# Attention, gated feed-forward and their product on one core: gate rows in free places, output weights split at the end, shared sums, and a doubled load of x

## The chip, the cores and the metric

The kernel runs on one core of a Trainium2 chip. Five engines work beside each other, each through its own queue of instructions in order: TensorE (PE, with weight loads shown apart as PEld), VectorE (DVE), ScalarE (ACT), GpSimd (POOL) and SyncE (SP), which here issues all DMA transfers. The metric is the device time of one execution in microseconds (us). Before the change it is 2596.14 us, the median of three runs (2592.55 to 2599.0).

## The reference

For x of 2048 tokens with D = 576 values, in float32:

```python
xn = _layernorm(x, axis=-1)
# attention, 32 heads of 18 values: wqkv is (576, 1728), wo is (576, 576)
q, k, v = ...(xn @ wqkv)
p = _softmax(einsum("bhqd,bhkd->bhqk", q, k) * 18 ** -0.5)
s = einsum("bhqk,bhkd->bhqd", p, v).reshape(B, S, D) @ wo
# feed-forward: w_gate and w_up are (576, 4608), w_down is (4608, 576)
y = (_gelu(xn @ w_gate) * (xn @ w_up)) @ w_down
return x + s * _silu(y)
```

## The kernel before

**Precision.** Operands of the matmuls have the type float32r; each is split into a high part and a low part (`split`, `split_ap`, `split_av`, `cut`: a copy gives the high part, a subtraction the low one), and a product is three matmuls: high by high, high by low, low by high.

**Stages.** A prologue normalizes x, transposes it, and projects queries, keys and values, four blocks of 512 tokens (`b`); it writes qk, vs and the transposed x (`xhs`, both parts) to DRAM. In its last block it also splits `wo` and stores the parts in DRAM as `wos` (`split_wo`, `store_wo`, L313 to L323). Then attention and feed-forward run interleaved. The feed-forward is cut into sections: one section is one slice of 128 of the 4608 inner columns for one block of 512 tokens, 27 pairs of matmuls (`gate_up`, L427; a pair is `pg` on partitions 0 to 63 and `pu` on 64 to 127). Two sections make a group `r` (`G` = 2, `NR` = 18 groups per block); after each group follows the down projection `py` (L538, 42 matmuls by a scheme with seven products), which DVE adds to `M` (L545). An attention section carries 8 slots beside the pairs: in each, a score product `pe` (L831) whose exponential ACT takes (L832), and for a later head group a product `pm` (L779) whose maximum DVE takes (L781). `pe`, `pm`, `py` and others share a ring of three PSUM buffers. After the section come 32 matmuls `acc` (L848) with the values.

**A change of block.** The pairs read the transposed x in three thirds of 192 rows, `xd[k]`, each as a high and a low tile, and need it on partitions 0 to 63 and again on 64 to 127. In the last section of a block `load_xd` (L144) loads the lower halves for the next block, and `copy_xd` copies them to the upper halves: ACT the high tiles (L151; the second and third thirds in three pieces each, between the exponentials of the next section), POOL the low tiles (L153). In the same place POOL forms sums of h and splits them (L465 to L467, L455, L456), which the down projection reads, and four pieces of T (the prepared down weights, `t_piece`, L483) are loaded.

**Scaling.** The attention's outputs lie unnormalized in DRAM (`oT`) with reciprocals `rT`. In free places of the attention, for one head group each time, `load_scale`, `scale` and `store_scale` load, multiply on POOL (L705) and store them as `on`. Two of the 32 are left to the end.

**The end.** After the attention five sections and three down projections remain. Among them stand 16 steps, one per 128 rows of the output: `project` (L991, 28 matmuls of the outputs with the parts of `wo`, result `po`), on DVE `multiply` (L1000, the gate row by po; L1005, plus x), then the store; then for a later row `split_o` (ACT `oh` L972, DVE `ol` L973 and L974) and `gate` (ACT tanh L982, DVE L983: y * (tanh(y/4) + 1), of which the product with 0.25 makes a gate, y being held doubled). Gate rows y of the first three blocks come from DRAM (`ys`), those of the last from `M`. `load_o` brings the normalized outputs of a block into KA.

**Order.** PE's instructions stand in the order of the code throughout; SP's from the attention on; ACT's, DVE's and POOL's in the end alone. Elsewhere a scheduler orders them when the program is built, except where `keep_in_program_order` holds one. `spread` places the slots and the `hooks` (work issued at a given pair) among a section's pairs.

Of the kernel before, what the change touches and what calls it, by code (L numbers as in the profile page):

```python
# [17 lines left out]
P = 128  # L18
# [3 lines left out]
KT = 4  # L22
# [30 lines left out]
PRODUCTS = ((2, (0, 6)), (5, (1, 3)), (3, (2, 5)), (6, (3, 4)), (0, (4, 2)), (4, (5, 1)), (1, (6, 0)))  # L53
QUARTERS = ((0, 0, 6), (0, 1, 4), (1, 0, 1), (1, 1, 5))
# [27 lines left out]
def kernel(ctx: ExitStack, tc: tile.TileContext, x, wqkv, wo, w_gate, w_up, w_down, out):  # L82
# [12 lines left out]
    wos = dram.tile([2, D, D], F32, name="wos")  # L95
# [70 lines left out]
    with tc.tile_pool(name="pro", bufs=1) as pro, tc.tile_pool(name="pps", bufs=1, space=PSUM) as pps:  # L166
# [102 lines left out]
        parts = []  # L269
# [42 lines left out]

        def split_wo(k):  # L313
            n = min(P, D - k * P)
            raw = raw_tile([P, D])
            tc.keep_in_program_order(nc.sync.dma_start(raw[0:n], wo[k * P:k * P + n, :]))
            hi, lo = (pro.tile([P, D], F32R, name=f"wo{i}", tag="rawp", bufs=5) for i in range(2))
            split(hi[0:n], lo[0:n], raw[0:n])
            return k, n, hi, lo

        def store_wo(k, n, hi, lo):
            for i, t in enumerate((hi, lo)):
                tc.keep_in_program_order(nc.sync.dma_start(wos[i, k * P:k * P + n, :], f(t)[0:n]))  # L323
# [33 lines left out]
        for b in range(NB):  # L357
            for n, t in enumerate(ORDER):
# [16 lines left out]
                if b == NB - 1 and 2 <= n < NK + 2:  # L375
                    store_wo(*parts.pop(0))
                if b == NB - 1 and n < NK:
                    parts.append(split_wo(n))
# [22 lines left out]
    FF = {"w": ahead, "xd": XD, "down": [], "gates": [], "n": 0, "hooks": {}, "next": {}, "raw": {},  # L401
# [169 lines left out]
    def section(specials=(), tag="f", slots=False, tail=0):  # L571
# [7 lines left out]
        hooks, FF["hooks"], FF["next"] = FF["hooks"], FF["next"], {}  # L579
# [48 lines left out]
    def finish():  # L628
# [8 lines left out]
        def hook(i, what, ahead="hooks"):  # L637
            FF[ahead].setdefault(i, []).append(what)

        def behind(what):  # L640
            if (n + 1) % (NR * G) == 0:
                hook(9, lambda: what(keep))
            else:
                what(lambda i: i)
# [23 lines left out]
        else:  # L668
            if g == 0:
                late = (n + 2) % (NR * G) == 0 and n + 2 < NF  # L670
                for k, i in enumerate((1, 6, 11, 16) if late else (None, 5, 13, 21)):
                    if i is None:
                        t_piece(r, k)
                    else:
                        hook(i, lambda k=k: t_piece(r, k), ("hooks", "next")[late])
# [17 lines left out]
    def load_scale(u):  # L693
# [3 lines left out]
        if not SC:  # L697
            SC.extend(ffn.tile([P, 2, TB], F32, name=m, tag=t) for m, t in (("on", "rawd"), ("od", "tsum")))
        nc.sync.dma_start(SC[0][:, u % 2], oT[g, :, cols])
        nc.sync.dma_start(SC[1][:, u % 2], rT[QD * g:QD * g + QD, cols].rearrange("h (o s) -> h o s", o=1).to_broadcast([QD, 32, TB]))  # L700

    def scale(u):

        o, d = (t[:, u % 2] for t in SC)
        nc.gpsimd.tensor_tensor(o, o, d, op=ALU.mult)  # L705

    def store_scale(u):

        j, g = divmod(u, NQ)
        for a in range(QD):  # L710
            row = (QD * g + a) * DH
            nc.sync.dma_start(on[j][row:row + DH, :], SC[0][32 * a + 1:32 * a + 1 + DH, u % 2])
# [9 lines left out]
    with tc.tile_pool(name="att", bufs=1, reuse_waits="tile") as att:  # L722
# [185 lines left out]
        scaled = 0  # L908
# [248 lines left out]
```

## Time and profile before

| | us |
|---|---|
| median of three runs | 2596.14 |
| profiled execution | 2595.73 |
| its span | 2593.9 |
| PE busy | 2554.1 (98%) |
| DVE busy | 2111.7 (81%) |
| POOL busy | 1599.7 (62%) |
| ACT busy | 1468.6 (57%) |

The span goes from the first to the last instruction; the profiled execution took 1.83 us more. Times of the trace count from the span's start. A row of the timeline is: start, duration, engine, line, operation, output and inputs, and in brackets how long the engine had been idle and what released it. Of the 2593.9 us the prologue and the first sections take about 340, the interleaved attention goes to about 2456, and the end takes the rest.

### The profile page before, as it was taken

Reading aid. Unit: us, or ns where it says so; the run is one execution under the profiler, and the core shown is the slowest. Engines: PE = TensorE matmul, PEld = TensorE weight load, DVE = VectorE, ACT = ScalarE, POOL = GpSimd, SP = SyncE. Lnnn points to the kernel's source line nnn. Section 1 sums busy time; section 2 is a strip of 40 time slices with the busy share of each in tenths; the row PEclk is TensorE's granted clock in tenths of the full one; section 3 lists DMA queues with packets and bytes.
Section 4 is the critical chain, followed back from the end, with each engine's and each line's share of the span. In section 5 each row is a group of like instructions: output and inputs, shape, how many; then the busy total and the mean of one; then the engine's idle time right before and its main releaser. Section 6 shows DMA issues by size and latency. Waiting matters only on the chain.

```text
span 2593.9 us, 52857 instructions
## 1 busy us (share of the span) xinstructions
PE 2554.1 (98%) x20548; PEld 1847.5 (71%) x20548; DVE 2111.7 (81%) x2399; ACT 1468.6 (57%) x1769; POOL 1599.7 (62%) x1679
## 2 busy tenths in 40 slices
PE   9999999999999999999999999999999999999988
PEld 8887766666666777666666676666666666676778
DVE  5325888888888888888878988888887888887377
ACT  3224366666666666555566655555566555556521
POOL 2115588888888855666667665555557655556641
PEclk9999999999999999999999999999999999999998
DMA  8865455555565566666666666666557665554683
GB/s 264 266 237 147 109 166 152 167 164 161 167 188 164 165 170 165 159 165 166 167 174 172 168 167 162 161 160 157 155 151 213 163 156 150 153 155 134 187 255 126
DMA packets 407880, 442.87 MB, mean 171 GB/s; under 512 B 106700, under 2 KB 286412, under 8 KB 407632
## 3 DMA queue, kind: packets, MB, share of 16 engines
q1 hardware_dynamic: 407632, 439.50, 61.6%
q8 instruction: 163, 2.67, 0.4%
q14 instruction: 85, 0.70, 0.1%
HBM read 344.12 MB, written 95.26 MB: 169 GB/s over the span
## 4 chain that ended last, share of the span: by engine, by line
PE 92%; DVE 2%; DMA 2%; POOL 1%; ACT 1%; issue 1%; SPq 1%; POOLq 0%; DVEq 0%; ACTq 0%
PE pg L427 27%; PE acc L848 17%; PE py L538 14%; PE pe L831 9%; PE pm L779 9%; PE po L187 7%; PE pu L427 7%; PE py L525 1%; PE po L991 1%; DMA raw<-in_B_w_up_dram 0%; DMA wol<-wos 0%; DVE mx L781 0%; DMA KA<-on 0%; PE pt L248 0%; DMA yy<-ys 0%
## 5 line engine op out<-in xcount | busy, mean ns | idle before, releaser
L832 ACT ACTIVATE pT<-pe 128x1024 f32<-128x1024 f32 x1024 | 1049.0, 1027 | 586.0 <-PE pe L831 551.1
L781 DVE TENSOR_REDUCE mx<-pm 128x2 f32<-128x1024 f32 x1024 | 1220.5, 1224 | 176.6 <-PE pm L779 161.8
L427 PE MATMUL pu<-xd,wh 64*128 64x512 f32 x2538 | 927.5, 397 | 6.5 <-POOL xd L153 4.9
L427 PE MATMUL pg<-xd,wh 64*128 64x512 f32 x2538 | 926.0, 396 | 1.9 <-ACT t L440 1.9
L427 PEld LDWEIGHTS pg<-xd,wh 64*128 64x128 f32 x2538 | 468.6, 185 | 123.7 <-issue 57.0
L427 PE MATMUL pg<-xd,wl 64*128 64x512 f32 x1269 | 496.4, 391 | 1.2 <-POOL wl L117 1.2
L427 PE MATMUL pu<-xd,wl 64*128 64x512 f32 x1269 | 495.9, 391 | 0.0
L427 PEld LDWEIGHTS pu<-xd,wh 64*128 64x128 f32 x2538 | 468.5, 185 | 24.4 <-POOL xd L153 5.7
L110 POOL TENSOR_SCALAR wh<-raw 128x384 fp32r<-128x384 f32 x402 | 215.4, 537 | 437.4 <-PE pu L427 333.4
L848 PE MATMUL acc<-pT,VS 128*32 128x512 f32 x4096 | 466.0, 595 | 0.0
L112 POOL TENSOR_TENSOR wl<-raw,wh 128x384 fp32r<-128x384 f32 x402 | 413.4, 1031 | 28.6
L779 PE MATMUL pm<-KA,QT 64*128 64x512 f32 x2048 | 416.5, 394 | 5.6 <-ACT pT L832 3.6
L831 PE MATMUL pe<-QT,KA 64*128 64x512 f32 x2048 | 412.5, 392 | 2.2 <-DVE mx L781 1.9
L538 PE MATMUL py<-T,ah 128*128 128x288 f32 x1876 | 385.9, 301 | 9.9 <-DVE yy L1000 7.0
L545 DVE TENSOR_TENSOR M<-py,M 128x576 f32<-128x576 f32 x448 | 338.8, 758 | 31.2 <-PE py L538 18.5
L538 PEld LDWEIGHTS py<-T,ah 128*128 128x128 f32 x1876 | 302.0, 190 | 65.9 <-issue 61.5
L456 POOL TENSOR_TENSOR al<-h,ah 128x512 fp32r<-128x512 f32 (+1 forms) x142 | 292.8, 2062 | 52.6 <-ACT ah L453 42.5
L848 PEld LDWEIGHTS acc<-pT,VS 128*32 128x32 f32 x4096 | 120.3, 109 | 276.5 <-issue 229.5
L538 PE MATMUL py<-T,al 128*128 128x288 f32 x938 | 277.8, 296 | 0.0
L831 PEld LDWEIGHTS pe<-QT,KA 64*128 64x128 f32 x2048 | 194.3, 184 | 113.0 <-DVE mx L781 26.2
L427 PEld LDWEIGHTS pg<-xd,wl 64*128 64x128 f32 x1269 | 234.4, 185 | 38.4 <-POOL wl L117 2.0
L427 PEld LDWEIGHTS pu<-xd,wl 64*128 64x128 f32 x1269 | 234.7, 185 | 8.3
(156 smaller groups left out, 2908.4 us busy)
## 6 DMA issues: line engine op xcount, KB each, us to landing
T<-ts SPq DMA_DIRECT2D x98, 576.0 KB
KA<-qk SPq DMA_DIRECT2D x768, 72.0 KB
T<-ts SPq DMA_DIRECT2D x98, 432.0 KB
raw<-in_B_w_gate_dram SPq DMA_DIRECT2D x144, 288.0 KB
raw<-in_B_w_up_dram SPq DMA_DIRECT2D x144, 288.0 KB
ts<-T SPq DMA_DIRECT2D x36, 576.0 KB
VS<-vs SPq DMA_DIRECT2D x128, 152.0 KB
qk<-t SPq DMA_DIRECT2D x72, 256.0 KB
```

Source lines behind the costliest of these rows:

```text
L110: first = nc.gpsimd.tensor_scalar(hi, raw, 1.0, 1.0, op0=ALU.mult, op1=ALU.mult)
L112: keep(nc.gpsimd.tensor_tensor(lo, raw, f(hi), op=ALU.subtract))
L187: nc.tensor.matmul(o, st, m, start=(i == 0), stop=(i == len(terms) - 1))
L427: nc.tensor.matmul(o, w[1 + wp][k][rr, c, :], xd[k][xp][rr, c, :], start=(i == 0), stop=(i == len(terms) - 1))
L456: keep(two.tensor_tensor(lo, raw, f(hi), op=ALU.subtract))
L538: nc.tensor.matmul(py[:, t, 0:DC], h[:, i, tt], T[:, w, k], start=n == 0, stop=n == 2)
L545: nc.vector.tensor_tensor(M[:, m], py[:, :, 0:DC], M[:, m], op=ALU.add)
L779: nc.tensor.matmul(pm[:, a], QS[u, r][rr, t * P:(t + 1) * P], KS[(u * NA + c) % KB][r][rr, :], start=True, stop=True)
L781: return nc.vector.tensor_reduce(MX[u][:, 2 * r:2 * r + 2, t, c], pm, axis=AX.X, op=ALU.max)
L831: nc.tensor.matmul(pe[:, a], KS[(u * NA + c) % KB][r][rr, t * P:(t + 1) * P], QS[u, r][rr, :], start=True, stop=True)
L832: nc.scalar.activation(PT[u, kt][:, 2 * r:2 * r + 2, :], pe, AF.Exp, scale=SCALE)
L848: nc.tensor.matmul(ACC[u][32 * a:32 * a + 32, :], VS[(u * NA + c) % VB][:, v:v + 32], pt[:, a, :], start=first, stop=last, skip_group_chec ...
```

## The change

1. **Output weights.** `wos` goes, with `split_wo` and `store_wo` in the prologue. At the end `load_wo` loads `wo` as it is into tiles that later hold x and gate rows, ACT copies the high parts, POOL subtracts the low ones.
2. **x at a change of block.** The last third is loaded twice, into both halves; its copies on ACT and POOL go. POOL's copies of the second third stand ahead of the sums of h, whose hook goes. Before the second and third change, two pieces of T are loaded ahead of x, two right behind it.
3. **Gate rows in the attention.** Where no scaling is ready, a place takes a gate row: load from `ys`, tanh on ACT, a multiplication and a sum on POOL, store to `ys`. Eleven of the twelve rows of the first three blocks are gated so; `gate` in the end does the twelfth.
4. **The end.** Both left scalings are loaded first and done in one place; x is loaded seven rows ahead; the sum with x goes to POOL in every second step up to the tenth; all pieces of T for the second down projection are loaded ahead of the steps. One projection moves from ahead of the last section to behind it: four, section, three, down, one, section, three, down, instead of four, section, three, down, two, section, two, down.

```diff
-    def load_xd(b, k):
+    def load_xd(b, k, halves=1):
             t = wts.tile([P, XG, TB], F32R, name=f"xd{i}_{k}")
-            nc.sync.dma_start(f(t)[0:HR], xhs[b][i, k * XG * HR:(k + 1) * XG * HR, :].rearrange("(k p) t -> p k t", p=HR))
+            for a in range(halves):
+                nc.sync.dma_start(f(t)[HR * a:HR * a + HR],
+                                  xhs[b][i, k * XG * HR:(k + 1) * XG * HR, :].rearrange("(k p) t -> p k t", p=HR))
...
         if new:
-            xd.append(load_xd(b + 1, NG - 1))
-            for k in range(1, NG):
-                for i in range(XG):
-                    FF["hooks"].setdefault(7 * k + 2 * i - 5, []).append(lambda k=k, i=i: copy_xd(xd[k], 0, keep, i))
-            for k in range(NG):
+            xd.append(load_xd(b + 1, NG - 1, 2))
+            for t in hooks.get(len(pairs), ()):
+                t()
+            for i in range(XG):
+                FF["hooks"].setdefault(2 + 2 * i, []).append(lambda i=i: copy_xd(xd[1], 0, keep, i))
+            for k in range(NG - 1):
                 for i in range(XG):
                     copy_xd(xd[k], 1, keep, i)
...
         def behind(what):
-            if (n + 1) % (NR * G) == 0:
-                hook(9, lambda: what(keep))
-            else:
-                what(lambda i: i)
+            what(keep if (n + 1) % (NR * G) == 0 else lambda i: i)
...
-                for k, i in enumerate((1, 6, 11, 16) if late else (None, 5, 13, 21)):
+                for k, i in enumerate((None, 5, 27, 27) if late else (None, 5, 13, 21)):
...
+    def gate(k, i):
+        y, t = (t[:, i] for t in SC)
+        nc.scalar.activation(t, y, AF.Tanh, scale=0.25)
+        nc.gpsimd.tensor_tensor(t, t, y, op=ALU.mult)
+        nc.gpsimd.tensor_tensor(y, y, t, op=ADD)
...
-            if FF["n"] % G == 1 and (scaled + 1) * NA + 4 < n and SCALED <= n < NU * NA - 2 and 2 < FF["n"] % (NR * G) < NR * G - 2:
-                load_scale(scaled)
-                at(n + 1, 2, scale, scaled)
-                at(n + 2, 0, store_scale, scaled)
-                scaled += 1
+            if FF["n"] % G == 1 and SCALED <= n < NU * NA - 2 and 2 < FF["n"] % (NR * G) < NR * G - 2:
+                done = scaled + gated
+                if (scaled + 1) * NA + 4 < n:
+                    jobs, k = (load_scale, scale, store_scale), scaled
+                    scaled += 1
+                else:
+                    jobs, k = (load_gate, gate, store_gate), gated
+                    gated += 1
+                jobs[0](k, done % 2)
+                at(n + 1, 2, jobs[1], k, done % 2)
+                at(n + 2, 0, jobs[2], k, done % 2)
...
         def load_wo():
-            nc.gpsimd.memset(f(OW[1])[HR:P, KT, :], 0.0)
-            for i, w in enumerate(OW):
-                nc.sync.dma_start(f(w)[:, 0:KT, :], wos[i, 0:R0, :].rearrange("(k p) n -> p k n", p=P))
-                for a in range(2 - i):
-                    nc.sync.dma_start(f(w)[HR * a:HR * a + HR, KT, :], wos[i, R0:D, :])
+            for i, t in enumerate(RAW[:KT]):
+                nc.sync.dma_start(t, wo[i * P:(i + 1) * P, :])
+            for a in range(2):
+                nc.sync.dma_start(RAW[KT][HR * a:HR * a + HR], wo[R0:D, :])
+
+        def split_wo():
+            wh, wl = OW
+            pool.memset(f(wl)[HR:P, KT, :], 0.0)
+            for i, t in enumerate(RAW):
+                act.activation(wh[:, i], t, AF.Copy)
+                rr = slice(0, P if i < KT else HR)
+                pool.tensor_tensor(wl[rr, i], t[rr], f(wh)[rr, i], op=SUB)
...
-            vec.tensor_tensor(xx, xx, t, op=ADD)
+            (pool if k % 2 and k < SHARED else vec).tensor_tensor(xx, xx, t, op=ADD)
```

`RAW` is `XX + YY[2:]`, three tiles for x and two for gate rows; `SHARED` is 11; `SC` holds the two buffers of the scaling, which the gate rows share.

ACT at the third change of block, before and after (`pT` are exponentials, `xd_1` and `xd_2` the second and third thirds of x, the numbers behind them those of the tiles):

```order
L852 ACTIVATE accs<-acc 128x512
L832 ACTIVATE pT<-pe 128x1024
L151 ACTIVATE xd_1_24419<-xd_1_24419 64x512
L832 ACTIVATE pT<-pe 128x1024
L151 ACTIVATE xd_1_24419<-xd_1_24419 64x512 x2
L832 ACTIVATE pT<-pe 128x1024
L151 ACTIVATE xd_2_24475<-xd_2_24475 64x512
L832 ACTIVATE pT<-pe 128x1024
L151 ACTIVATE xd_2_24475<-xd_2_24475 64x512 x2
L832 ACTIVATE pT<-pe 128x1024 x4
```

```order
L853 ACTIVATE accs<-acc 128x512
L833 ACTIVATE pT<-pe 128x1024
L153 ACTIVATE xd_1_24397<-xd_1_24397 64x512
L833 ACTIVATE pT<-pe 128x1024
L153 ACTIVATE xd_1_24397<-xd_1_24397 64x512 x2
L833 ACTIVATE pT<-pe 128x1024 x6
```

Three of six copies between the exponentials are gone; the other three stay where they were.

POOL at the second change of block, before and after (`h` are the activations whose sums and splits `ah`, `al` the down projection reads; `wh` and `wl` the split weights of later sections):

```order
L153 COPY xd_0_16593<-xd_0_16593 64x512 x3
L465 TENSOR_TENSOR h_16682<-h_16436,h_16682 128x512
L466 TENSOR_TENSOR h_16682<-h_16436,h_16682 128x256
L467 TENSOR_TENSOR h_16682<-h_16682 128x256
L455 TENSOR_SCALAR ah<-h_16682 128x1280
L456 TENSOR_TENSOR al<-h_16682,ah 128x1280
L153 COPY xd_1_16636<-xd_1_16636 64x512 x3
L110 TENSOR_SCALAR wh<-raw 128x384
L112 TENSOR_TENSOR wl<-raw,wh 128x384
L153 COPY xd_2_16692<-xd_2_16692 64x512 x3
```

```order
L155 COPY xd_0_16550<-xd_0_16550 64x512 x3
L155 COPY xd_1_16593<-xd_1_16593 64x512 x3
L450 TENSOR_TENSOR h_16639<-h_16391,h_16639 128x512
L451 TENSOR_TENSOR h_16639<-h_16391,h_16639 128x256
L452 TENSOR_TENSOR h_16639<-h_16639 128x256
L110 TENSOR_SCALAR wh<-raw 128x384
L440 TENSOR_SCALAR ah<-h_16639 128x1280
L112 TENSOR_TENSOR wl<-raw,wh 128x384
L441 TENSOR_TENSOR al<-h_16639,ah 128x1280
```

The copies of the second third went ahead of the sums, those of the last third are gone. In the attention, ten of the eleven tanh (`od<-on`) stand behind the fourth or fifth of a section's eight exponentials, one ahead of the first.

DVE in the end, two steps between the second section and the second down projection, before and after (`yy` gate rows, `po` the projection, `xxs` rows of x, `ol` and `oh` parts of a later step's outputs):

```order
L1000 SCALAR_TENSOR_TENSOR yy_31013<-yy_31013,po 128x576
L1005 TENSOR_TENSOR xxs<-xxs,yy_31013 128x576
L973 TENSOR_TENSOR ol<-KA,oh 128x512
L974 TENSOR_TENSOR oh<-KA,oh 64x128
L983 SCALAR_TENSOR_TENSOR yy_31015<-th,yy_31015 128x576
L1000 SCALAR_TENSOR_TENSOR yy_31014<-yy_31014,po 128x576
L1005 TENSOR_TENSOR xxs<-xxs,yy_31014 128x576
L973 TENSOR_TENSOR ol<-KA,oh 128x512
L974 TENSOR_TENSOR oh<-KA,oh 64x128
L983 SCALAR_TENSOR_TENSOR yy_31012<-th,yy_31012 128x576
```

```order
L1015 SCALAR_TENSOR_TENSOR yy_31015<-yy_31015,po 128x576
L990 TENSOR_TENSOR ol<-KA,oh 128x512
L991 TENSOR_TENSOR oh<-KA,oh 64x128
L1015 SCALAR_TENSOR_TENSOR yy_31016<-yy_31016,po 128x576
L1020 TENSOR_TENSOR xxs<-xxs,yy_31016 128x576
L990 TENSOR_TENSOR ol<-KA,oh 128x512
L991 TENSOR_TENSOR oh<-KA,oh 64x128
```

The gate's operation left DVE, and of two sums one.

More of the change, by code (lines that the diff above doesn't have):

```diff
@@ L398 @@
     ps = ctx.enter_context(tc.tile_pool(name="ps", bufs=1, space=PSUM, reuse_waits="tile"))
[L401 removed]
+    FF = {"w": ahead, "xd": XD, "down": [], "gates": [], "n": 0, "hooks": {}, "raw": {},
           "M": ffn.tile([P, 7, 2, DC], F32, name="M"),
@@ L1011, in step @@
             split_o(n + 2)
-            gate(n + 2)
-            load_xy(n + 4)
+            b, j = groups[min(n + 2, len(groups) - 1)]
+            if b < 2 and j == TB // P - 1:
+                load_o(b + 2)
             for t in pieces[:2]:
@@ L1016, in step @@
             del pieces[:2]
+            load_y(n + len(YY))
+            load_x(n + len(XX))
             n += 1
+            if ahead:
+                gate(n + 1)
         def load_raw(n):
@@ L1061 @@
         todo.pop("rec")[0]()
-        split_o(0)
+        for i, u in enumerate(rest):
+            load_scale(u, i)
+        load_wo()
+        for k in range(2):
+            load_y(k)
+        load_raw(first + 3)
         end()
@@ L1091 @@
         cut_a(1, h1, pool, pool)
-        gate(1)
+        load_raw(first + 4)
         for m in ("rawd", "tsum"):
@@ L1095 @@
             XX.extend((t[:, 0], t[:, 1]))
-        load_xy(3)
-        for k in range(2):
-            step()
-        load_raw(first + 4)
-        for k in range(2):
+        for t in pieces:
+            t()
+        del pieces[:]
+        for k in range(3, len(XX)):
+            load_x(k)
+        for k in range(4):
             step()
@@ L1103 @@
         end()
-        for k in range(3):
+        for k in range(2):
             step()
+        step(False)
         last_down(1)
+        gate(n + 1)
         sums_a(0, h, pool)
         cut_a(0, h, pool, pool)
-        for k in range(2):
-            step()
+        step()
         h, end = last_section("f")
```

115 lines of the change are left out of this document (51 added, 64 removed).

## The prediction

> **What bounds the kernel.** First the page's engine table, then the stages of the program with each engine's busy time (columns: stretch, length, busy PE, PEld, DVE, ACT, POOL, granted clock, DMA share, GB/s), then two pieces of the chain that ended last.
>
> ```profile
> PE 2554.1 (98%) x20548; PEld 1847.5 (71%) x20548; DVE 2111.7 (81%) x2399; ACT 1468.6 (57%) x1769; POOL 1599.7 (62%) x1679
> ...
> 150.00:220.00 70.00, 68.85 (x440) 58.63 (x439) 21.66 (x29) 21.37 (x40) 30.49 (x31) 1.00 0.69 219
> ...
> 713.33:751.29 37.96, 34.92 (x279) 23.43 (x279) 29.44 (x30) 27.41 (x33) 30.87 (x34) 1.00 0.78 207
> ...
> 1319.86:1360.41 40.55, 36.85 (x279) 25.96 (x279) 29.19 (x30) 25.38 (x30) 24.37 (x31) 0.92 0.70 179
> ...
> 1925.35:1961.61 36.26, 34.48 (x280) 23.79 (x279) 29.75 (x30) 25.30 (x30) 23.33 (x29) 1.00 0.77 196
> ...
> 2456.37:2594.00 137.63, 118.17 (x845) 108.04 (x844) 101.50 (x135) 29.61 (x44) 41.79 (x38) 0.93 0.63 198
> ```
> ```profile
> 1286.62 5.74 PE py L538 x42
> 1319.86 5.74 PE py L538 x42
> ```
>
> TensorE is the bound: 2554 of 2593.9 us. In the attention the chain returns to the same down projection every 33.24 us, and PE is busy throughout. What is not PE stands in few places: the three changes of token block, called T1, T2 and T3 here, where such a period takes 37.96, 40.55 and 36.26 us, thus 4.7, 7.3 and 3.0 above 33.24; and the last 137.6 us, where PE rests for 19.5 and runs part of the time at a lower granted clock (0.93 on average). So a cost on another engine counts only where PE then waits, and a gain only in those four places.
>
> **Prologue: nothing.** Five splits of the output weights on POOL, ten stores and five loads go. The row 150 to 220 above holds them; PE rests 1.15 us there in all. That is the most to be had; the waits in it stand behind ACT copies whose order does not change, so I take 0 (0 to 1).
>
> **Block changes: 10.6 us.** Two causes stand in the rows: at T2 POOL, at T3 ACT.
>
> ```profile
> 1340.29 1.29 POOL L465 TENSOR_TENSOR h<-h,h 128x512 f32<-128x512 f32 x1 [1.01 <-DVE h L444]
> ...
> 1344.41 2.88 POOL L456 TENSOR_TENSOR al<-h,ah 128x1280 fp32r<-128x1280 f32 x1
> 1347.36 1.73 POOL L153 CAST xd<-xd 64x512 fp32r<-64x512 f32 x3
> ...
> PE pu L427 <- POOL xd L153: 3.6, 1, 3.6
> ```
> ```profile
> 1945.73 1.03 ACT L832 ACTIVATE pT<-pe 128x1024 f32<-128x1024 f32 x1 [0.23 <-PE pe L831]
> 1946.78 0.63 ACT L151 ACTIVATE xd<-xd 64x512 fp32r<-64x512 f32 x1
> ...
> 1956.03 2.14 ACT L832 ACTIVATE pT<-pe 128x1024 f32<-128x1024 f32 x2 [0.48 <-PE pe L831]
> ```
> ```profile
> 1646.42 2.12 ACT L832 ACTIVATE pT<-pe 128x1024 f32<-128x1024 f32 x2 [2.04 <-PE pe L831]
> ...
> 1651.32 2.13 ACT L832 ACTIVATE pT<-pe 128x1024 f32<-128x1024 f32 x2 [0.22 <-PE pe L831]
> 1653.89 2.16 ACT L832 ACTIVATE pT<-pe 128x1024 f32<-128x1024 f32 x2 [0.44 <-PE pe L831]
> ```
>
> At T2 the copies of the second third of x stand on POOL behind the sums and splits of h, 1340.29 to 1347.3, and PE waits 3.6 us for them. In the new order both groups of copies precede the sums. At T3 six copies between the exponentials (3.6 us at 0.6 each) put the seventh exponential 10.30 us behind the first, against 7.47 in an undisturbed section: 2.83 us later, so that ACT hands on all but 0.75 us of what is put between. Three copies remain, 1.8 us, of which I let 1.2 through. So T3 falls from 3.0 to 1.2, T2 from 7.3 to 1.2.
>
> The last third now comes by four transfers in place of two. What that costs the queue:
>
> ```profile
> 1936.00:1947.00 11.00, 11.00 (x97) 6.92 (x95) 8.82 (x10) 9.69 (x12) 6.43 (x11) 1.00 1.02 212
> ...
> xd<-xhs SPq DMA_DIRECT2D x24, 384.0 KB
> ```
>
> Six loads of 384 KB fill the queues for 11 us at 212 GB/s, 1.86 us each. Two more shift the end from about 1947.3 to 1951, with some 2 us to the signal 1953. PE's section there starts at about 1945.0 (the first exponential, 1945.73, needs its first product); two thirds in, with 1.2 us of delay, it asks for the low part at 1953.6 (6.6 us of pairs, two pairs more). So the cover is about 0.6 us at T3, 1 at T2 by the same count, and at T1, where stores of T share the queues, it is gone by 0.8: T1 falls from 4.7 to 2.0. Gain 2.7 + 6.1 + 1.8 = 10.6. Bounds: 12 if the halves load at once, 4 if the last third comes 2 us later still at each change. [...]
>
> Two pieces of T's high part now go ahead of the x loads and two right behind; they had been late at T2 and T3 without a wait of PE, so 0. The sums of h lose a hook and stand behind the copies: at T2 their splits end at 1347.3, one group of copies (1.73) moves ahead of them, and the down that reads them is the one at 1360.41: 0.
>
> **Gating in the attention: a loss of 2.5 us.** Eleven times: one load and one store of 288 KB, a tanh on ACT, two POOL operations. Order: ten tanh stand among the eight exponentials of a section, one ahead of them.
>
> ```profile
> L982 ACT ACTIVATE th<-yy x12: 667/686/692, 2480.9 to 2557.1; 128x576 f32<-128x576 f32 x12
> ...
>   DMA od<-rT: 4.4, 4
> ```
> ```profile
> 747.64 1.43 POOL L490 TENSOR_TENSOR tsum<-rawd 128x576 f32<-128x576 f32 x1
> ...
> 1637.04 1.30 POOL L705 TENSOR_TENSOR on<-on,od 128x512 f32<-128x512 f32 x1
> 1642.20 0.99 POOL L110 TENSOR_SCALAR wh<-raw 128x384 fp32r<-128x384 f32 x2 [3.86 <-PE pu L427]
> ```
>
> A tanh takes 0.69 us. Behind the fourth exponential ACT has 0.22 us free, and 0.44 two later; the fifth ends about 0.5 late. Between nothing (the 0.75 that T3 absorbed) and 0.69 on PE I take 0.25, by the nearest row, the slack at 1651.32: ten times, 2.5 us (0 to 7). POOL: 2.9 us where a multiplication at 1637.04 had 3.86 us free behind it: hidden, and without that cover the next weight splits, not needed for a section, are late. SP's queue: the store waits for POOL half a period after it, nothing is late behind it. In 30 such loads before, POOL waited 4.4 us in all (the row of the tile "on"), so I add no wait for data.
>
> **The end: 14 us.** The stretches of the end, and the chain's price of a projection:
>
> ```profile
> 2456.40:2481.10 24.70, 24.12 (x198) 19.94 (x199) 17.44 (x22) 6.31 (x10) 7.96 (x10) 1.00 1.07 296
> 2481.10:2502.10 21.00, 17.70 (x122) 17.30 (x121) 16.21 (x19) 4.82 (x8) 16.20 (x15) 0.92 0.53 162
> 2502.10:2521.40 19.30, 17.83 (x139) 16.18 (x139) 12.66 (x17) 4.79 (x8) 5.32 (x6) 1.00 1.07 350
> 2521.40:2536.50 15.10, 8.97 (x46) 8.19 (x45) 13.32 (x17) 2.00 (x3) 5.21 (x5) 0.77 0.66 219
> ```
> ```profile
> 2536.49 7.42 PE po L991 x56
> ```
> ```profile
> 2496.84 0.40 PE L991 MATMUL po<-woh,ol 128*128 128x288 f32 x1 [3.30 <-DVE ol L973]
> 2528.28 0.82 PE L538 MATMUL py<-T,ah 128*128 128x288 f32 x2 [4.68 <-DVE yy L1000]
> ```
> ```profile
> 2550.36 0.60 ACT L1040 ACTIVATE h<-pg 128x512 f32<-128x512 f32 x1 [5.10 <-PE pg L427]
> ```
> ```profile
> 2495.04 1.75 DVE L973 TENSOR_TENSOR ol<-KA,oh 128x512 fp32r<-128x512 f32 x1
> ...
> 2556.59 1.49 DVE L456 TENSOR_TENSOR al<-h,ah 128x1280 fp32r<-128x1280 f32 x1 [1.34 <-ACT ah L453]
> 2558.01 0.75 DVE L1000 SCALAR_TENSOR_TENSOR yy<-yy,po 128x576 f32<-128x576 f32 x1
> 2558.79 0.76 DVE L1005 TENSOR_TENSOR xx<-xx,yy 128x576 f32<-128x576 f32 x1
> 2559.46 0.68 DVE L973 TENSOR_TENSOR ol<-KA,oh 128x512 fp32r<-128x512 f32 x1
> 2560.16 0.28 DVE L974 TENSOR_TENSOR oh<-KA,oh 64x128 fp32r<-64x128 f32 x1
> 2560.48 0.76 DVE L983 SCALAR_TENSOR_TENSOR yy<-th,yy 128x576 f32<-128x576 f32 x1
> ```
>
> A projection is 7.42 / 2 = 3.71 us, a down projection 5.74, a section (24.12 - 5.74) / 3 = 6.1. From 2481.1 to 2536.5 PE has seven projections, one section and one down: 26.0 + 6.1 + 5.7 = 37.8 us of work in 55.4, so 17.6 are lost, most of it behind DVE. Per step DVE now does 0.75 + 0.76 + 0.68 + 0.28 + 0.76 = 3.2 us alone and more beside POOL (1.75 for 0.68). The last 0.76 goes for 11 of 12 rows, and every second sum up to the tenth step goes to POOL: 1.7 and 2.5 us per step, below PE's 3.71. What stays: about 2 us where DVE runs beside POOL (first four steps), and 1 in the second down projection, whose first sums wait for a step. So 17.6 falls to about 3.6: 14 us.
>
> The split of the raw weights must fit ahead of the first projection at 2481: 1.44 MB lands, after 1 MB for the scales and the T pieces, at about 2471 at the 296 GB/s of that row or better; ACT 5 x 0.69 from there, POOL 5 x 1.43 beside it, end about 2480. Bounds 0 to 3 us of loss; I take 0, as wol's POOL price is a row, and count 3 in the range. POOL's sums of rows 1 and 3 stand behind its splits of h, near 2496; SP's load of the third block of outputs (KA) waits behind the first of them, until about 2497, and is needed only after three more projections and a section: 0.
>
> From 2536.5 to 2570 the third projection now follows the last section. DVE's chain after that section ends with al 7.7 us behind it (2550.3 to 2558.0); then multiplication, sum and split (0.75 + 0.76 + 0.68) give the fourth projection its operand some 20 us after the down, where PE would be ready at 17.3. T's last pieces come behind the store of the same step, at about 24. Both put the down's start at 24, where it began at 21 but stood half done until 25.6: gain 0 (-3 to +3).
>
> **Rivals.** First, DVE stays the bound of the end: ol and its companion 3.0 us beside POOL in each of seven steps gives 0.75 + 0.38 + 3.0 = 4.1 or, with doubled sums, 4.5 us against 3.71, 5.6 us more, and 2 for late weights: 2582. For it speaks 1.75 against 0.68, against it that POOL is free in half the steps. [...] Second, the last third of x lands late at all three changes: the waits of PE stay by half, gain 4, 2580. Third, slower: tanh waits for its load, and the exponentials queue behind it on ACT, then PE. At 22 us of net gain it takes 3.0 us per gate, ten times, to come out 7.8 us above: 2604. Four waits in 30 loads speak against it. Fourth, both first rivals and full tanh prices together leave less than 7.8 us: 2592.
>
> **Numbers.** 10.6 - 2.5 + 14 = 22 us. The profiled execution took 2595.73 us (span 2593.9 and 1.8 around it), 0.4 below the median of the runs: 2574. Forecast 0.60, first rival 0.16, second 0.10, third 0.06, fourth 0.08. The range goes from full gains (2564) to both rivals (2588). 0.3% is 7.8 us, about what runs of this kernel differ by (2592.6 to 2599.0): faster 0.86, same 0.08, slower 0.06.
>
> **What would show it.** Periods at the changes of about 35.2, 34.4 and 34.4 us; PE waits for POOL's copies gone at T2; sections with a tanh 0.25 longer; the down of 2521 some 14 earlier, with no PE wait above 2 us for yy; the clock at 1.00 there. Wrong if the period in the attention grows by over 0.5 us, or if PE waits for woh or wol.

## The result, and the profile after

The changed kernel takes 2580.95 us, median of four runs (2580.15 to 2582.14), against 2596.7 for the kernel before beside it (2592.55 to 2599.0): a ratio of 0.9941, 95% interval 0.9924 to 0.9959, 15.75 us less. Forecast were 2574 and a range of 2564 to 2588. The profiled execution after took 2580.15 us, with a span of 2578.4, which is 15.5 below the span before.

The span divides best at the down projections, since each period of the attention starts with one. First their starts in the chain of work that ended last, for the kernel after (start, duration, engine, product, line), then the two starts before that the prediction did not show:

```profile
714.35 5.74 PE py L523 x42
749.18 5.74 PE py L523 x42
786.49 5.74 PE py L523 x42
1318.51 5.74 PE py L523 x42
1353.47 5.74 PE py L523 x42
1919.05 5.74 PE py L523 x42
1953.82 5.74 PE py L523 x42
2443.67 5.79 PE py L523 x42
```
```profile
787.79 5.74 PE py L538 x42
2450.60 5.79 PE py L538 x42
```

| piece of the span | before | after | gain | forecast |
|---|---|---|---|---|
| start to T1 | 713.33 | 714.35 | -1.0 | 0 |
| T1 | 37.96 | 34.83 | 3.1 | 2.7 |
| the period behind T1 | 36.50 | 37.31 | -0.8 | 0 |
| T2 | 40.55 | 34.96 | 5.6 | 6.1 |
| T3 | 36.26 | 34.77 | 1.5 | 1.8 |
| rest of the attention (T1 to T2, T2 to T3, T3 to its last down) | 1586.00 | 1587.45 | -1.5 | -2.5 |
| the end, from the attention's last down | 143.3 | 134.7 | 8.6 | 14 |
| sum | | | 15.5 | 22 |

The last row but one is the one that missed. The stretches of the end after the change (columns as in the prediction):

```profile
2449.40:2468.00 18.60, 18.60 (x164) 15.10 (x163) 12.51 (x15) 4.96 (x8) 8.74 (x11) 1.00 0.98 271
2468.00:2481.30 13.30, 7.72 (x46) 7.49 (x45) 8.12 (x9) 4.41 (x7) 12.97 (x13) 0.74 0.78 215
2481.30:2503.90 22.60, 21.48 (x168) 19.71 (x166) 16.34 (x18) 2.96 (x4) 16.66 (x15) 1.00 0.94 317
2503.90:2522.36 18.46, 17.20 (x130) 16.96 (x129) 14.57 (x20) 3.45 (x5) 6.09 (x6) 1.00 0.76 239
2522.36:2552.92 30.56, 27.76 (x208) 25.29 (x207) 20.90 (x30) 5.92 (x8) 3.79 (x2) 1.00 0.47 163
```

In the second stretch, the first down projection of the end, PE works 7.72 of 13.3 us, at a granted clock of 0.74 (the share of TensorE's full clock that the profile shows as granted). Before, PE's longest wait in that down was 0.43 us. In the other four PE is busy for 85.0 of 90.2 us, and the old waits, 3.30 for `ol` and 4.68 for `yy`, are gone. What PE, ACT and DVE do around the new hole, from the timelines of the kernel after:

```profile
2476.19 0.85 PE L523 MATMUL py<-T,ah 128*128 128x288 f32 x2 [5.58 <-DVE M L530]
```
```profile
2467.29 2.05 ACT L968 ACTIVATE woh<-xx 128x576 fp32r<-128x576 f32 x3 [0.79 <-DMA xx<-in_A_wo_dram]
```
```profile
2471.56 1.79 DVE L990 TENSOR_TENSOR ol<-KA,oh 128x512 fp32r<-128x512 f32 x1 [3.61 <-ACT oh L989]
```
```profile
2461.44 8.69 DMA yy<-in_A_wo_dram
...
2470.80 0.73 ACT oh L989
2471.56 1.79 DVE ol L990
...
2475.47 0.68 DVE M L530
2476.19 3.92 PE py L523 x15
```

The last fence is the chain, in order of time. The down projection writes into a ring of three PSUM buffers, which DVE empties into M (L530). DVE stands still for 3.61 us ahead of that, because `split_o(1)` precedes the sums in its queue and waits for ACT's `oh` (L989); the split itself then takes 1.79 and 1.39 us. ACT has `oh` queued behind five copies of `woh`, and these wait for `wo` from DRAM. So a load that nobody needs before 2481 stops PE at 2470.6: it is passed on through the order of two queues. ACT's step on the gate of the same section (L1060) is behind the copies as well.

### The profile page after: what moved, and what is told of

The parts are those of the page before. It is cut to its first block, busy times and chain, and to the rows that moved or that the text cites. A ratio compares the mean times of both kernels' runs of the same rounds, so it can differ in the third digit from the quotient of the medians.

```text
span 2578.4 us, 52876 instructions
## 1 busy us (share of the span) xinstructions
PE 2545.5 (99%) x20548; PEld 1838.7 (71%) x20548; DVE 2105.1 (82%) x2383; ACT 1464.1 (57%) x1765; POOL 1630.5 (63%) x1692
## 4 chain that ended last, share of the span: by engine, by line
PE 95%; DVE 3%; DMA 1%; ACT 1%; POOL 1%; issue 0%; SPq 0%; DVEq 0%; POOLq 0%; ACTq 0%
PE pg L412 26%; PE acc L849 18%; PE py L523 15%; PE pm L780 9%; PE pe L832 9%; PE pu L412 8%; PE po L189 7%; PE po L1006 1%; PE py L510 1%; PE pt L250 0%; DVE mx L782 0%; DMA yy<-in_A_wo_dram 0%; DVE ol L990 0%; DVE M L530 0%; DMA od<-rT 0%
## 5 line engine op out<-in xcount | busy, mean ns | idle before, releaser
L782 DVE TENSOR_REDUCE mx<-pm 128x2 f32<-128x1024 f32 x1024 | 1220.9, 1224 | 167.5 <-PE pm L780 151.9
L530 DVE TENSOR_TENSOR M<-py,M 128x576 f32<-128x576 f32 x448 | 338.7, 758 | 30.4 <-PE py L523 17.6
```

Of the source, the lines that this page charges most:

```text
L530: nc.vector.tensor_tensor(M[:, m], py[:, :, 0:DC], M[:, m], op=ALU.add)
L782: return nc.vector.tensor_reduce(MX[u][:, 2 * r:2 * r + 2, t, c], pm, axis=AX.X, op=ALU.max)
```

## Experiments

Each was run beside the kernel before on its chip; the four groups had medians of 2596.7 to 2598.34 for that.

### Move one split behind the down

```diff
         split_wo()
-        split_o(1)
         for k in range(3):
             load_x(k)
...
         last_down(0)
         end()
+        split_o(1)
         gate(0)
```

> The changed kernel with the split of the second outputs (split_o(1)) moved behind the first down projection. Theory: in the changed kernel DVE adds the first products of that down to M only after split_o(1), which waits for ACT, which waits for the weights wo; PE stands 5.58 us in the middle of the down. With the split behind, that wait falls below 0.5 us, and the time from 2581 to about 2576 (2575 to 2577.5). Rival: the weights themselves are late (their transfer, or POOL's subtractions), so the same microseconds are lost a little later, at the first or second projection: 2580 to 2582.

```profile
2472.88 0.53 PE L523 MATMUL py<-T,ah 128*128 128x288 f32 x2 [1.54 <-DVE M L530]
```
```profile
2468.70:2476.35 7.65, 6.11 (x46) 5.88 (x45) 4.84 (x7) 3.32 (x6) 7.34 (x7) 1.00 0.80 152
```

Median 2579.73 us (2575.56 to 2582.2), ratio 0.9929 (0.9914 to 0.9943). In the profile the wait falls from 5.58 to 1.54, not below 0.5, and the end (from 2444.40 of 2573.5) from 134.7 to 129.1: the whole expected 5.6. Of that, 4.0 us are wait; another 1.6 come because PE's own work in this down falls from 7.72 us at a clock of 0.74 to 6.11 at 1.00. No wait of PE comes at the first projections, so the weights are not late for them, and the rival falls. The times of whole executions do not show it: the median is only 1.2 us below that of the changed kernel, the two intervals overlap, and only the profiled execution meets the expected range. So this gain rests on one profile, until the better order below. What is known of the spread stands under "The period behind T1". The rest of 1.54 is ACT's step on the gate, still behind the copies of `woh`.

### No gate rows in the attention

```diff
-                else:
-                    jobs, k = (load_gate, gate, store_gate), gated
-                    gated += 1
```

(The loads, jobs and stores then stand under the condition for scaling.)

> The changed kernel without gate rows in the attention: the places only scale, and the end gates all twelve rows (tanh on ACT, one DVE operation each). Theory: in the attention 1.5 us come back (the eleven periods with a gate took 0.14 us more each); in the end DVE has 0.76 us more in each of eleven steps, 3.2 us alone and about 4 beside POOL against PE's 3.71, so that PE waits there some 5 to 8 us more: 2585 to 2588. Rival: DVE keeps enough room in the end without the gates having been moved; then only the attention's part shows: 2579 to 2580.

Median 2585.89 us (2583.78 to 2588.99), ratio 0.9955 (0.994 to 0.997). Between T2 and T3 and from T3 to the last down the profile has 565.12 and 489.34 us, against 565.58 and 489.85 with the gates: 1.0 us in all for eleven gates. The end takes 139.9 us against 134.7, so 5.2 more. Its waits, as the profile lists them from the first down on (total, times, longest):

```profile
PE py L523 <- DVE M L530: 9.2, 3, 5.5
```
```profile
PE py L523 <- DVE M L530: 7.5, 3, 5.6
```

The first is without, the second with the gates in the attention. These waits make 1.7 of the 5.2 us. By the stretches, 3.8 stand between the ends of the first and the second down, where PE is also busy 1.8 us longer: behind a wait of 2.64 us for `M`, groups of three matmuls of `py` follow each other every 0.72 us (2521.40 to 2524.28) in place of 0.39. By the profile, moving the gates is worth 4.2 us net, and the mechanism of the prediction (DVE is what the end waits for) holds.

### One load of the last third

```diff
-            xd.append(load_xd(b + 1, NG - 1, 2))
+            xd.append(load_xd(b + 1, NG - 1))
...
-            for i in range(XG):
-                FF["hooks"].setdefault(2 + 2 * i, []).append(lambda i=i: copy_xd(xd[1], 0, keep, i))
-            for k in range(NG - 1):
+            for k in range(1, NG):
+                for i in range(XG):
+                    FF["hooks"].setdefault(7 * k + 2 * i - 5, []).append(lambda k=k, i=i: copy_xd(xd[k], 0, keep, i))
+            for k in range(NG):
```

> The changed kernel with the last third of x loaded once at a change of block, its copies on ACT and POOL back, ACT's high copies at their old places; POOL's copies still stand ahead of the sums of h. Theory: the doubled load gives the gain at T1 and T3 (copies gone from between the exponentials), the order on POOL the gain at T2; periods of about 37, 36 and 36 us instead of 34.8, 35.0 and 34.8, so 4 to 5 us slower: 2585. Rival: the order on POOL alone brings it all, the loads being neutral: 2580 to 2582. Second rival: the two half loads run one after the other and cost what they save at T1; then T1 gets faster here, below 34.8.

```profile
715.75:751.99 36.24, 34.49 (x280) 23.17 (x279) 29.10 (x30) 27.39 (x33) 27.30 (x31) 1.00 0.81 211
1323.45:1359.81 36.36, 34.61 (x279) 23.23 (x279) 29.01 (x30) 25.22 (x30) 22.87 (x28) 1.00 0.82 202
1925.64:1961.80 36.16, 34.36 (x279) 23.45 (x279) 29.12 (x30) 25.27 (x30) 21.79 (x27) 1.00 0.82 203
```

Median 2587.31 us (2586.61 to 2588.52), ratio 0.996 (0.9945 to 0.9975). The three changes take 36.24, 36.36 and 36.16: the second load is worth 1.4 us at each, 4.2 in all. The step from before to here is the order on POOL with the pieces of T: 1.7, 4.2 and 0.1. Both edits that the prediction counted on are there, and each has its own part. The second load takes copies from ACT and POOL together, so the run does not separate these two. In the wait list of T3, PE's waits for exponentials ("PE pm <- ACT pT") are two of 0.8 us here, and one of 0.8 with the doubled load.

### The changes of block alone

The kernel before, with the edits of `load_xd`, `section`, `behind` and the pieces of T in `finish` as the diff has them, and nothing else.

> The kernel before with only the changes of block edited (last third loaded twice, POOL's copies ahead of the sums of h, T's pieces beside x); prologue, attention places and end as before. Theory: the three periods fall to 34.8, 35.0 and 34.8 us as in the changed kernel, 10.2 us in all, and nothing else moves: 2587 to 2589 against 2598. Rival: part of it is given back in the period behind the first change: then its excess over 33.24 grows from the 3.3 us before, and the time is 2590 to 2594.

```profile
714.93:749.84 34.91, 34.04 (x280) 23.61 (x279) 29.07 (x30) 25.61 (x30) 26.38 (x29) 1.00 0.82 206
749.84:787.44 37.60, 34.12 (x279) 22.77 (x279) 35.80 (x38) 21.84 (x25) 35.36 (x34) 1.00 0.69 210
1319.53:1354.58 35.05, 34.14 (x280) 23.46 (x279) 28.96 (x30) 23.46 (x27) 21.07 (x25) 1.00 0.89 214
1920.21:1954.99 34.78, 33.84 (x280) 23.52 (x279) 29.07 (x30) 23.49 (x27) 19.05 (x23) 1.00 0.90 217
```

Median 2589.52 us (2587.25 to 2594.8), ratio 0.997 (0.9957 to 0.9984), 8.3 us by the medians. The three periods add up to 104.74 against 114.77 before: 10.0 us. The period behind T1 is 37.60, where before it was 36.50, so 1.1 go back there in this profile, as the rival had it; but this period varies by more than that between profiles of one kernel (below). The median lies between theory and rival.

### Sums with x on DVE alone

```diff
-SHARED = 11
+SHARED = 0
```

> The changed kernel with all sums with x on DVE (SHARED = 0). Theory: DVE has 0.76 us more in five steps, 2.5 us alone but up to 3.5 beside POOL's splits; three of those steps stand where PE already waits for ol: 2 to 4 us slower, 2583 to 2585. Rival: an operation on POOL slows DVE by as much as it takes off it, so sharing is worth nothing: 2580 to 2582.

Median 2582.09 us (2581.34 to 2584.37), ratio 0.9938 (0.9922 to 0.9955), which cannot be told from the changed kernel. In the profile the end takes 136.4 us (from 2445.95 of 2582.3), 1.7 more. I expected 2 to 4; sharing is worth at most 1.7, and the times alone would not show it.

### The weights' parts from the prologue

`split_wo` and `store_wo` in the prologue and the load of both parts in the end, as before the change; the rest of the change stays.

> The changed kernel with the output weights split in the prologue and loaded as two parts, as before the change; all else of the change stays. Theory: with no copies of woh ahead of split_o(1) on ACT and no subtractions of wol on POOL, the wait in the first down projection falls from 5.58 to below 1.5 us, and the prologue costs 0 to 1 us more: 2575 to 2578. Rival: the two parts are twice the bytes (2.88 MB for 1.44), land later, and PE waits for them ahead of the first projection of the end as long as it now waits in the down: 2580 to 2583.

```profile
2480.97 0.40 PE L1015 MATMUL po<-wol,oh 128*128 128x288 f32 x1 [1.59 <-DMA wol<-wos]
...
2518.54 0.50 PE L541 MATMUL py<-T,ah 128*128 128x288 f32 x2 [1.71 <-DVE yy L1024]
2522.34 0.85 PE L541 MATMUL py<-T,ah 128*128 128x288 f32 x2 [2.77 <-DVE M L548]
```
```profile
2514.84 0.75 DVE L1024 SCALAR_TENSOR_TENSOR yy<-yy,po 128x576 f32<-128x576 f32 x1 [3.58 <-DMA yy<-ys]
```

Median 2583.7 us (2581.09 to 2585.83), ratio 0.9944 (0.9931 to 0.9956). The changed kernel, run again beside it, took 2582.64 (2580.98 to 2587.62), ratio 0.9945 (0.9932 to 0.9957). My theory missed. The first down is nearly free of waits, as expected, but the end takes 135.0 us (from 2448.69 of 2583.7), as long as with the raw weights: PE now waits 1.59 us for `wol` at the first projection, less than the rival had it, and then 1.71 and 2.77 for DVE in the second down. DVE in its turn had waited 3.58 us for the load of a gate row. So the split on chip as such costs no more than the stored parts do; with the first experiment, what cost was its place in the queues.

### Every tanh three times

```diff
-        nc.scalar.activation(t, y, AF.Tanh, scale=0.25)
+        for _ in range(3):
+            nc.scalar.activation(t, y, AF.Tanh, scale=0.25)
```

> The changed kernel with each tanh of the attention done three times in a row (same result, 1.38 us more on ACT for each of eleven gates). Theory: one tanh costs PE about 0.1 us because ACT has 0.2 to 0.5 us free behind each pair of exponentials and catches up within a section; three exceed that room at first, PE waits about 0.7 us more per gate: 2587 to 2590. Rival: three PSUM buffers and the pairs of the feed-forward between the slots let ACT fall behind by over 2 us without a wait: 2580 to 2582.

The chain of this kernel, then of the changed one, across one period with a gate:

```profile
1654.30 5.74 PE py L523 x42
1688.64 5.74 PE py L523 x42
```
```profile
1652.68 5.74 PE py L523 x42
1685.98 5.74 PE py L523 x42
```

Median 2592.57 us (2589.57 to 2597.46), 9.9 above the changed kernel in the same group. The period takes 34.34 us in place of 33.30; without a gate it takes 33.24. So a gate with one tanh of 0.69 us costs PE 0.06, and of the 1.38 us of two more PE pays 1.04. The theory's kind is right, but its 0.7 per gate and its 2587 to 2590 were too low. ACT's room there is, as an estimate from these periods, 0.6 us (one tanh of 0.69 less the 0.06 that PE pays) to 1 us (three of 2.07 in all less 1.10); what exceeds it PE pays.

### The end in a better order

Two kernels go on from the first experiment. In the first of them DVE splits ahead of its multiplication in each step, and the split of the step ahead of the second and third down stands behind that down's sums:

```diff
-            multiply(n, project(n))
-            split_o(n + 2)
+            po = project(n)
+            if not late:
+                split_o(n + 2)
+            multiply(n, po)
...
-        step(False)
+        step(False, True)
         last_down(1)
+        split_o(n + 1)
```

> The kernel with split_o(1) behind the first down projection, and two edits of the same kind: in each step the split of a later row stands ahead of the multiplication on DVE, and in the step ahead of the second and of the third down projection it stands behind that down's sums. Theory: PE's waits of 2.0 and 1.25 us for ol and of 1.3 and 1.0 us for M fall to about 0.5 each: 4 us less than with split_o(1) alone, 5.6 + 4 below the changed kernel: 2571 to 2573. Rival: DVE has the same work in the same time; the waits only move to po and to the tail, where the sum with x is the last thing: 2575 to 2577.

```profile
2542.92 0.61 PE L523 MATMUL py<-T,ah 128*128 128x288 f32 x1 [2.88 <-DMA T<-ts]
```

Median 2579.16 us (2575.95 to 2582.86), ratio 0.993 (0.9916 to 0.9943). Behind the first down the waits for `ol` and `M` shrank to 0.4 to 1.6 us, but the first down's is 2.43 in place of 1.54 with the same code up to there, and the end took 132.8 us (from 2443.77 of 2576.6), 3.7 more than with the first edit alone. Neither theory nor rival had the reason: T's pieces for the third down are loaded behind the stores of the steps, a later multiplication makes these stores late, and now T is late, 2.88 us. The second kernel loads T earlier:

```diff
         split_o(n + 1)
         gate(n + 1)
+        for t in pieces:
+            t()
+        del pieces[:]
...
             act.activation(t1, pg, AF.Square)
+            if mid:
+                mid()
+                for k in range(3):
+                    split_gu(nxt, k)
```

Here `mid` issues the fourth and fifth copy of `woh` with their subtractions, and behind them the loads of x and gate rows that stood there; the first three copies stay ahead of ACT's squares.

> The version with all three splits moved, and two more edits: ACT squares the last of the first three sections' gates ahead of the fourth and fifth copy of woh, so that DVE's sums of the first down don't wait for it; and all pieces of T for the third down projection are loaded ahead of the steps, as for the second. Theory: the waits of 2.43 (first down) and 2.88 us (third down, for T) fall below 0.5 each; from the last down of the attention to the end 128 us or less, where the changed kernel has 134.7: 2573 to 2576. Rival: the weights are late next, and PE waits 1 to 2 us at the first projections: 2576 to 2578.

```profile
2468.60:2475.20 6.60, 5.99 (x45) 5.76 (x44) 5.01 (x8) 4.11 (x7) 6.46 (x7) 1.00 0.80 189
```
```profile
2471.78 0.53 PE L523 MATMUL py<-T,ah 128*128 128x288 f32 x2 [0.61 <-DVE M L530]
```

Median 2573.18 us (2571.23 to 2573.71), ratio 0.9905 (0.9891 to 0.9919): faster than both kernels. The changed kernel beside its own before had 0.9945 (0.9932 to 0.9957). The end takes 125.2 us (from 2444.23 of 2569.4), 9.6 below the changed kernel, and the first down has 0.61 us of wait in place of 5.58, little above the 0.5 expected, at a clock of 1.00. The third down no longer waits for T, but 1.08 us for DVE's `yy`. Nothing waits for the weights. Here the times show what the first experiment's did not: all four lie below all nine of the changed kernel (2580.15 to 2587.62).

### The period behind T1

A repeat of the changed kernel showed that the period behind T1 is not the same in each execution. The profile of the repeat:

```profile
749.16:791.14 41.98, 36.05 (x280) 24.85 (x279) 39.06 (x38) 21.83 (x25) 35.48 (x34) 0.92 0.59 186
```

> The changed kernel unaltered, beside the others of this group on one chip: 2580 to 2582 us. It also tells how far one execution's places repeat: the start, the period behind the first change of block (36.5 to 39.5 us in the five profiles so far), and the wait of 5.58 us in the first down projection of the end.

The repeat took 2582.64 us, 0.6 above the expected range. Its end agrees with the first profile: 134.8 us against 134.7, with a wait of 5.71 against 5.58. The period behind T1 does not: it took 37.31 in one profile and 41.98 in the other, of kernels with the same instructions. The first of DVE's four sums of M with M in that period, and POOL beside it, in the repeat, and PE's wait behind them; then the same sum in the kernel of the first experiment, whose period took 36.63:

```profile
758.64 6.34 DVE L542 TENSOR_TENSOR M<-M 128x576 f32<-128x576 f32 x1
```
```profile
758.87 1.47 POOL L542 TENSOR_TENSOR M<-M 128x576 f32<-128x576 f32 x1
760.25 0.84 POOL L493 TENSOR_TENSOR T<-tsum,T 128x288 fp32r<-128x288 f32 x1
761.00 1.44 POOL L494 TENSOR_TENSOR T<-rawd,T 128x576 fp32r<-128x576 f32 x1
762.35 1.45 POOL L542 TENSOR_TENSOR M<-M 128x576 f32<-128x576 f32 x1
```
```profile
766.18 0.79 PE L832 MATMUL pe<-QT,KA 64*128 64x512 f32 x2 [5.92 <-DVE mx L782]
```
```profile
757.92 0.75 DVE L542 TENSOR_TENSOR M<-M 128x576 f32<-128x576 f32 x1
```

It took 6.34 us or 0.75. In the long case it ends only behind four POOL operations that read two SBUF operands each. DVE's maxima (L782) queue behind it, and PE waits 5.92 us for those. In twelve profiles with these four DVE sums, their total goes from 4.4 to 9.0 us and the period from 36.50 to 41.98, nearly in the same order. An attempt to take DVE's sums away:

```diff
-            one = nc.vector if b == 0 else nc.gpsimd
+            one = nc.gpsimd
```

> The same, and behind the first change of block the sums of M with M on POOL alone, in place of four on DVE. Theory: the period behind the first change takes 36.6 to 42 us, differently in each execution, since one of DVE's sums (0.75 us alone, up to 6.34) cannot get in between POOL's, and DVE's maxima and PE wait behind it; with none on DVE the waits for mx go, the period repeats, and POOL's four sums of 1.44 us delay the weight splits instead: 35 to 38 us, so a spread of the times below 3 us in place of 7. Rival: the spread comes from the loads, then it stays as wide and the period varies as before.

```profile
780.57 0.79 PE L832 MATMUL pe<-QT,KA 64*128 64x512 f32 x2 [5.15 <-DVE mx L782]
```
```profile
779.20 0.21 DVE L802 STREAM_TRANSPOSE mt<-m 128x32 f32<-128x32 f32 x1 [5.33 <-POOL m L797]
```

Median 2576.85 us (2576.41 to 2579.59), 3.7 above the kernel without this edit in the same group, and the period is 40.09, beyond my 35 to 38. POOL's own queue is the reason: a small operation on the maxima (L797) now stands behind its four added sums, DVE waits 5.33 us for it and PE 5.15 for DVE. The spread of the times was 3.2 us, but that of the kernel without the edit was 2.5, so the run does not tell where the spread comes from. That the long DVE sum makes the long period is read from the timeline; that it makes the whole spread of the times is not shown.

## Why the prediction was right, and where it was not

The sign, the order of the terms and the range hold; the sum was 6.5 us too good (22 forecast, 15.5 measured).

**The end, 14 forecast, 8.6 measured**, is the mis-sized term. The step that failed is "Bounds 0 to 3 us of loss; I take 0" for the split of the raw weights. I looked for its cost at the first projection at 2481, the reader of the weights. There was none. The cost came at 2470.6, in the down that doesn't read them: a wait of 5.58 us, through ACT's copies ahead of `oh` and `split_o(1)` ahead of DVE's sums. By stretches, from the start of the attention's last down to the end of each down of the end, and on to the last instruction:

| stretch of the end | before | after | gain | forecast | gain with the split moved |
|---|---|---|---|---|---|
| to the end of the first down | 31.55 | 37.64 | -6.1 | 0 | -0.4 |
| to the end of the second | 54.34 | 41.05 | 13.3 | 14 | 14.7 |
| to the end of the third | 33.53 | 30.56 | 3.0 | 0 | 1.6 |
| to the last instruction | 23.88 | 25.44 | -1.6 | not looked at | -1.6 |
| sum | 143.3 | 134.7 | 8.6 | 14 | 14.2 |

So the step taken at 0 cost 6.1 us, beyond its bounds, and the 14 was nearly right where it was forecast: the prediction let 3.6 us of loss stay there, and 3.2 stayed (41.05 less 37.8 of work). The waits of 3.30 and 4.68 us are gone. That the second down ends at 2522.36 in place of 2536.49, 14.1 earlier, looks like the forecast sign but is chance: the attention's last down already stood 6.9 earlier. With the split moved, the profile's end takes 129.1 us, 14.2 below before, as forecast; that the third and fourth rows cancel there is luck. The load of `wo` landed at 2470.13, about when the prediction had it (2471), but the 2471 was counted against an end that began 6.9 us later; the prediction's own gains had moved the deadline. What an earlier landing would have saved was not tried.

**Block changes, 10.6 forecast, 10.2 measured.** The periods are 34.83, 34.96 and 34.77 (forecast 35.2, 34.4, 34.4), and the doubled load and the order on POOL have separate parts, as the third experiment shows. At T2, PE's wait of 3.6 us for POOL's copies is gone from the wait list. The doubled load was feared most at T1; no wait of PE for x's transfers is in the wait lists of the three periods, and removing it made each 1.4 us longer. Here the pair pays, because it takes copies from ACT and POOL while the transfers have cover. That two more loads cost 3.7 us was an estimate from the 1.86 us of each load before; while the eight loads at T3 went out the queues moved 226 GB/s (1930 to 1943), with the six before 212, and whether the two of a pair run one after the other is not shown by these runs. The 2 us to the signal in the count of the cover were an estimate too: before, POOL's copies of the second third started at 1945.61, released by the load, 2.2 us after the fourth of the six loads would have ended at 1.86 us each (1943.4).

**The period behind T1, 0 forecast, -0.8 measured**, was no term at all. With the edits of the changes alone it was 1.1 longer. But it varies by 4.7 us between two profiles of one kernel, so neither its cause nor its part in the 6.5 is settled. The same holds for the start: 1.0 us later here, 347.7 to 350.2 for the first such down in all profiles, without an order by prologue.

**Gating, 2.5 forecast, 1.0 to 1.5 measured.** The choice between 0 and 0.69 per gate was right in kind; the 0.25 taken was some 0.1. ACT's room is 0.6 us or more, as the triple tanh shows, not the 0.44 I read behind one pair of exponentials.

**The rivals.** Of the first, that DVE stays the bound of the end, half is true: PE waited for DVE, but most by the order of one queue at one place. DVE's work per step still made PE wait, 1.12 and 1.26 us between the first and the second down, but not the 5.6 of the rival. The last third did not land late, and no tanh waited in a way that PE felt (33.30 us against 33.24).

**Of what would show it**, the periods came within 0.6 us, and the clock was 1.00 in the second down. The fall of the clock in the first down (0.74) and its wait stood in no sign; I had written "wrong if PE waits for woh or wol", and the wait I should have named was for M.

## What to carry to other kernels

When a load or a split moves closer to its use, look at what is queued behind it on every engine that it passes, and not at its reader alone: the first to wait may be an operation that doesn't use it (here the first down, 5.58 us). In a queue that keeps its order, as DVE's does in this end, an operation that waits for a transfer belongs behind the sums that free a ring of PSUM buffers: of the 9.6 us of the better order, 5.6 stand in the profile of that edit alone. And an edit that delays one engine's last step can delay the stores behind it, and the loads that share their queue (2.88 us here). A deadline for a load moves with the gains ahead of it (6.9 us here): count it in the new kernel's times.

## What the runs showed of the hardware

One DVE operation with two SBUF inputs, 0.75 us with POOL at rest (773.36 in the repeat), took up to 6.34 us beside POOL operations of the same kind, and not each time: the same instruction took 1.43 and 6.34 us in two profiles of one kernel. In the long case an earlier POOL operation (756.23, 2.73 us) was still running when it started. The DVE sum ended at 764.98, behind the four POOL operations that followed (758.87 to 763.80). In the kernel of the first experiment the same sum started 0.06 us ahead of a POOL sum (757.92 and 757.98) and took 0.75, and that POOL sum took 1.97 us, where the changed kernel has 1.43. That DVE's sum gets no turn between POOL's operations in the long case is my reading of the rows; what decides it was not tried.

After a stall PE ran at a lower granted clock in one profile and not in another. In the kernel of the first experiment a projection behind a wait of 2.05 us ran at 0.68; in the changed kernel the same projection behind the same wait ran at 1.00:

```profile
2536.00:2541.20 5.20, 5.19 (x28) 5.19 (x29) 3.79 (x5) 0.00 (x0) 1.79 (x1) 0.68 0.94 323
```
```profile
2542.30:2546.00 3.70, 3.65 (x27) 3.61 (x27) 3.59 (x5) 0.00 (x0) 1.82 (x1) 1.00 0.91 290
```

That is 1.5 us for a projection, so of a stall's price a part is not in the wait itself. In the last kernel of the better order the clock of the stretch from 2514 to 2545.3 was 0.95: there groups of three matmuls of `py` followed each other every 0.72 us from 2541.41 to 2544.29, in place of 0.39, behind waits of only 1.08 and 0.40 us. What decides it was not tried.
